# Recurrence, router, experts and a feed-forward layer on one core: the last products of two steps in one run over two column groups

## The chip, the cores and the metric

The kernel runs on one core of a Trainium2 chip. The metric is the device time of one execution in microseconds (us). The core has a matrix engine (TensorE: PE in the rows, and PEld for its weight loads), VectorE (DVE), ScalarE (ACT), GpSimd (POOL) and SyncE (SP), which issues most DMAs. Each engine works through a queue of its own in order; semaphores order the queues against each other.

## The reference, cut to what matters

```python
B, H, S, D = 4, 8, 768, 40
for t in range(S):                     # attention-like recurrence, one 40x40 state per (b, h)
    y[:, :, t] = einsum('bhd,bhde->bhe', r[t], state)
    Sa = einsum('bhde,bhe->bhd', state, a[t])
    state = state * w[t] - outer(Sa, b[t]) + outer(v[t], k[t])
x = y as (3072 tokens, 320)
# mixture of 8 experts: argmax of x @ w_gate picks one; relu(x @ w1[e]) @ w2[e], times the gate
# then a feed-forward layer: h = x @ w_in; maximum(0.01 h, h) @ w_out
```

All of it is in float32 (the weights of the last layer come in float64).

## The kernel before, in words

The program has two parts, one behind the other. The first, `attention`, computes the recurrence in chunks of 32 time steps, and the router's choice for every token. The second, `moe`, computes the experts and the last layer with a written-out order of its own; it is not touched here.

The 768 time steps are cut into 6 blocks (`i`), each of 2 halves (`hf`) of 4 chunks (`g`) of 32. What the code calls a step `s` (0 to 47) is one chunk of one half: `s = 8 i + 2 g + hf`. The two halves are steps of even and odd number; they work on different batches, so that their states don't depend on each other: step `s` needs the state of step `s - 2`. One step treats 16 sequences, as 8 pairs (`p`, with `j` for the member of the pair).

For every chunk `load` brings k, b, a and w, `prep` scales them by running products of w, `gram` makes the 32x32 products within a chunk, `inverse` inverts the triangular matrices of a whole block on VectorE (after a round through DRAM: the copies `mab` are stored in `Md` and loaded as `Mu`), `back` brings the result in as `TB`, and `fix` completes it with many tiny products (lines 488 and 497). `turn` transposes the decays into `Wt` (line 397). A step itself consists of these parts:

- `rv` loads r into a buffer `RE` and v into a buffer `MV`.
- `kbt` transposes k and b (line 524) into `NI` and copies them into the state buffer `Z` as well.
- `chain` is the path from state to state: products at line 554, a copy into X, products at line 565, copies into MV, products at line 581, and the new state into MV of step `s + 2` (line 585).
- `output` transposes MV (line 601) into `Z`, makes r's products with keys (line 614), masks them into `RE` (line 622), and then makes the chunk's rows of y: 16 products, 32 columns wide in weights, 40 wide in the moving operand (line 633, called the py products here). Their results lie in `py`, three PSUM banks; chunk `g` has partitions 32 g to 32 g + 31. Where `g` is 3, the four chunks of a half are complete: VectorE weights them with `Wt` into two of the four buffers `xb` (line 645), and `R.add` routes these 256 tokens: transposes (line 843), logits (854), softmax and places on VectorE, and two scatters on GpSimd (889) that write the tokens into their expert's region `xs`.

The columns of the array that a product uses follow from its output partitions. The 16 py products of a step all use the same group of 32 columns; line 554 puts its products on four such groups in turn, line 581 on the two halves of the partitions in turn.

The order of all this is not the order of the code. Every piece is handed to a planner (`Sched.op`) with a duration, the keys that it reads and writes, and a due time; `Sched.run` places the pieces on the five queues one by one, by its own model of the engines, and `emit` writes them out in that order. Where the planner sees a gap on TensorE, it inserts fillers (line 743: products of constants into an unused corner of `py`), in number a share of the gap. The numbers of buffers (`NRE` for RE, `NZ` for Z, `NWT` for Wt) enter through the keys: a piece that writes a buffer waits for all who read its last content.

Of the kernel before, what the change touches and what calls it, by code (L numbers as in the profile page):

```python
# [239 lines left out]
NMV, NRE, NNI, NZ, NWT = 6, 7, 2, 3, 6  # L240
# [38 lines left out]
def attention(ctx, tc, I, R, eng):  # L279
# [53 lines left out]
    maskZ = cp.tile([TW, XC], F32, name="maskZ")  # L333
# [110 lines left out]
    def inverse(i, parts=(0, 1)):  # L444
# [4 lines left out]
        kM, kT, kt = [[(x, h) for h in parts] for x in ('Mu', 'Tt', 'tmp')]  # L449
# [143 lines left out]
    def output(s):  # L593
# [22 lines left out]
        for j in range(2):  # L616
# [10 lines left out]
            if pm:  # L627
                op('P', .62, lambda E, o=o, j=j: E.tensor_tensor(RE[o:o + 64, j], RE[o:o + 64, j], maskP[o:o + 64].unsqueeze(1).broadcast_to([64, 8, 32]), ALU.mult), ['mask'], [('REs', s % NRE, j, par) for par in range(2)])
        def fy(E):
            for p in range(8):  # L630
                for j in range(2):
                    b, col = place(hf, 2 * p + j)
                    E.matmul(py[32 * g:32 * g + 32, b, col:col + 40], RE[:, j, p, :], Z[:, p, ZC[j]:ZC[j] + 40], start=True, stop=True)  # L633
        op('T', 1.28, fy, zo + [('Zs', s % NZ, j) for j in range(2)] + [('REo', s % NRE, j) for j in range(2)] + [('REs', s % NRE, j, par) for j in range(2) for par in range(2)], [('py', hf, g)], banks=[('py', b) for b in ((0, 1), (1, 2))[hf]], act=2030)
        if g == 3:
            xk = []
            for bb in range(2):
                x = (2 * n + bb) % R.NXB
                xk.append(x)
                u = 8 * bb  # L640
                while u < 8 * bb + 8:
                    b, col = place(hf, u)
                    m = min(8 * bb + 8 - u, 12 - col // 40)
                    op('V', .15 + .0416 * m, lambda E, x=x, u=u, b=b, col=col, m=m, bb=bb:
                       E.tensor_tensor(R.xbs[x][:, 40 * (u - 8 * bb):40 * (u - 8 * bb) + 40 * m], py[:, b, col:col + 40 * m], Wts[n % NWT][:, u:u + m, :].rearrange("p h e -> p (h e)"), ALU.mult),  # L645
                       [('py', hf, k) for k in range(4)] + [('Wt', n % NWT, h, j) for h in range(2) for j in range(2)], [('xb', x, u)], banks=[('py', b)])
                    u += m
            Q.spare = SPF
            R.add(Q, psum, copy, ev, hf, i, xk)
            Q.spare = SPO  # L650
# [50 lines left out]
    for i in range(6):  # L701
# [22 lines left out]
        for c in range(8):  # L724
# [8 lines left out]
            if i == 0 and c < 4:  # L733
                Q.since = ZR0 + ZRS * c
                for e in (2 * c, 2 * c + 1):
                    R.zero_region(Q, e, maskZ, [('X', s % 2)])
# [3 lines left out]
            output(s)  # L740
            Q.spare = 0.
# [27 lines left out]
class Router:  # L769
# [4 lines left out]
    def __init__(self, ctx, tc, I, eng, capacity):  # L774
# [16 lines left out]
        self.tok = cp.tile([128, 1], I32, name="tok")  # L791
# [22 lines left out]
    def setup(self):  # L814
# [4 lines left out]
        P.iota(self.tok, [[0, 1]], base=0, channel_multiplier=1)  # L819
# [10 lines left out]
    def add(self, Q, psum, copy, ev, hf, blk, xk):  # L830
# [55 lines left out]
        for i, x in enumerate(xk):  # L886
            op('P', .18, lambda E, i=i, x=x: E.tensor_scalar(self.xbs[x].bitcast(I32)[:, D:D + 1], self.tok, (2 * hf + i) * 768 + blk * 128, None, ALU.add), ['rconst'], [('xbt', x)])
# [558 lines left out]
```

## Time and profile before

| what | us |
|---|---|
| median of 3 runs (1145.17 to 1154.86) | 1154.43 |
| the profiled execution | 1154.42 |
| its span, first to last instruction | 1152.6 |
| TensorE busy, fillers included | 1037.0 |
| VectorE / ScalarE / GpSimd busy | 729.0 / 553.9 / 303.9 |
| fillers (line 743), 1161 of them | 82.8 |
| first load of scattered tokens issued, the end of the recurrence | 560.28 |

The profile is that of one execution. Busy times are of the whole span; a stretch of it can look quite different. Matrix records come in pairs of a weight load and a product, and a product in float32 has two records of each kind.

### The profile page before, as it was taken

To read this page: it belongs to the slowest core of one execution; us is meant where nothing else is said; L and a number is where in the kernel's file an instruction comes from. 1 tells how busy PE (TensorE), PEld (TensorE's weight loads), DVE (VectorE), ACT (ScalarE), POOL (GpSimd) and SP (SyncE) were. 2 spreads that over 40 slices of the span, in tenths; PEclk is the share of its full clock that TensorE was granted. 3 is DMA by queue.
4 is the path that set the end of the run, shared out by engine and by line. 5 is a ranking of instruction groups with operands and counts; after the bars stand their busy time and mean duration, and the time that the engine had idled before them with its cause. 6 is when DMAs were issued, how large, how long until landed. Compare 5 with 4: busy or idle time off the path is not lost.

```text
span 1152.6 us, 39205 instructions
## 1 busy us (share of the span) xinstructions
PE 1037.0 (90%) x17036; PEld 929.2 (81%) x17036; DVE 729.0 (63%) x1613; ACT 553.9 (48%) x1269; POOL 303.9 (26%) x279
## 2 busy tenths in 40 slices
PE   5786987998978989899589999999999999999997
PEld 4675776887866877778579889889989999999997
DVE  8884684985966955434477787786764545444453
ACT  5133654855836836667344434444533333333343
POOL 6000011002002001010145565673749191010100
PEclk9988897998989979989799999999999999999999
DMA  7757566464554722430466666653311010000000
GB/s 182 200 142 191 144 143 196 135 138 142 130 141 125 184 61 72 96 96 6 142 213 197 190 196 201 203 175 122 92 35 49 21 36 12 12 14 10 24 13 15
DMA packets 146244, 129.59 MB, mean 112 GB/s; under 512 B 102288, under 2 KB 110736, under 8 KB 146064
## 3 DMA queue, kind: packets, MB, share of 16 engines
q1 hardware_dynamic: 143760, 119.11, 37.6%
q0 software_dynamic: 2304, 7.89, 1.9%
q8 instruction: 136, 2.23, 0.8%
q14 instruction: 44, 0.36, 0.1%
HBM read 102.13 MB, written 24.85 MB: 110 GB/s over the span
## 4 chain that ended last, share of the span: by engine, by line
PE 55%; issue 17%; DVE 8%; ACT 8%; DMA 6%; POOL 4%; SPq 2%; DVEq 0%; POOLq 0%; ACTq 0%
PE ph L1000 13%; PE py L633 5%; PE py L743 4%; PE ch L581 3%; PE tr L601 3%; ACT Z L297 3%; PE oy L1207 2%; PE oy L1206 2%; PE oy L1205 2%; PE tr L397 2%; PE tr L415 2%; PE tr L497 2%; DMA wc<-cvm 2%; PE tr L614 2%; ACT NI L297 2%
## 5 line engine op out<-in xcount | busy, mean ns | idle before, releaser
L1000 PE MATMUL ph<-xt,wq 128*128 128x512 f32 (+2 forms) x1408 | 311.8, 365 | 4.9 <-DVE xt L1041 4.9
L1000 PEld LDWEIGHTS ph<-xt,wq 128*128 128x128 f32 x1408 | 248.4, 190 | 35.0 <-DVE xt L1041 6.0
L1185 DVE TENSOR_TENSOR gf<-gf,ph 128x512 f32<-128x512 f32 (+1 forms) x112 | 68.3, 610 | 99.0 <-ACT gf L1184 92.6
L889 POOL DMA_INDIRECT xs<-xb,rii x24 | 28.8, 1199 | 371.6 <-DVE rii L879 260.8
L1189 DVE TENSOR_TENSOR gl<-gf,gh 128x512 fp32r<-128x512 f32 (+1 forms) x112 | 76.7, 685 | 70.0 <-ACT gh L1188 70.0
L1184 ACT ACTIVATE gf<-ph 128x512 f32<-128x512 f32 (+1 forms) x112 | 60.0, 535 | 109.6 <-PE ph L1000 107.0
L1188 ACT CAST gh<-gf 128x512 fp32r<-128x512 f32 (+1 forms) x112 | 62.7, 559 | 96.4 <-DVE gf L1185 95.0
L297 ACT COPY Z<-tr 40x512 f32<-40x512 f32 (+1 forms) x192 | 97.7, 539 | 20.9 <-PE tr L601 19.1
L1051 ACT ACTIVATE gh<-ph 128x448 fp32r<-128x448 f32 x64 | 34.9, 545 | 118.7 <-PE ph L1000 118.7
L1207 PE MATMUL oy<-wo,gl 128*128 128x320 f32 x288 | 89.2, 310 | 0.1
L1206 PE MATMUL oy<-wo,gh 128*128 128x320 f32 x288 | 88.9, 309 | 0.0
L1205 PE MATMUL oy<-wo,gh 128*128 128x320 f32 x288 | 88.8, 308 | 0.0
L743 PE MATMUL py<-one 128*128 128x128 bf16 x1161 | 82.8, 224 | 3.2 <-DVE xb L645 1.6
L1215 POOL DMA_INDIRECT out_dram<-ob,gid x24 | 23.9, 995 | 218.5 <-ACT ob L1214 213.3
L622 DVE TENSOR_TENSOR RE<-tr,maskP 64x128 f32<-64x128 f32 x192 | 55.1, 287 | 35.6 <-PE tr L614 28.0
L585 DVE TENSOR_TENSOR MV<-ch,WC 40x320 f32<-40x320 f32 x92 | 44.9, 488 | 50.3 <-PE ch L581 42.6
L743 PEld LDWEIGHTS <-one 128*128 128x128 bf16 x1161 | 69.9, 100 | 8.0 <-issue 3.6
L1065 PE MATMUL y<-gh,wo 128*128 128x448 f32 x192 | 73.1, 381 | 2.9 <-DVE Y L1072 2.9
L633 PE MATMUL py<-Z,RE 128*32 128x40 f32 x1536 | 69.9, 212 | 2.1 <-issue 2.1
L1068 PE MATMUL y<-gl,wo 128*128 128x448 f32 x192 | 70.6, 368 | 0.0
L633 PEld LDWEIGHTS py<-Z,RE 128*32 128x32 f32 x1536 | 64.3, 120 | 5.9 <-issue 2.7
L430 DVE TENSOR_TENSOR AE<-tr,maskP 32x128 f32<-32x128 f32 x176 | 49.9, 284 | 28.6 <-PE tr L415 17.8
(170 smaller groups left out, 2140.8 us busy)
## 6 DMA issues: line engine op xcount, KB each, us to landing
KB<-in_kbT_dram SPq DMA_DIRECT2D x24, 512.0 KB
RE<-in_rT_dram SPq DMA_DIRECT2D x48, 256.0 KB
AE<-in_aT_dram SPq DMA_DIRECT2D x20, 512.0 KB
raw<-in_wo_dram SPq DMA_DIRECT2D x16, 640.0 KB
raw<-in_wqa_dram SPq DMA_DIRECT2D x16, 512.0 KB
w<-in_wT_dram SPq DMA_DIRECT2D x24, 264.0 KB
xs<-maskZ SPq DMA_DIRECT2D x8, 563.5 KB
win<-xs SPq DMA_DIRECT2D x8, 563.5 KB
```

The lines of the kernel that those rows point to most:

```text
L297: (E.copy if E is A else E.tensor_copy)(o, i)
L633: E.matmul(py[32 * g:32 * g + 32, b, col:col + 40], RE[:, j, p, :], Z[:, p, ZC[j]:ZC[j] + 40], start=True, stop=True)
L743: Q.emit(lambda: T.matmul(py[:, 2, 320:448], R.one, R.one, start=True, stop=True))
L1000: T.matmul(ph, l, r, start=k == 0, stop=k == 7)
L1065: T.matmul(y[c], hi, gh, start=m == 0, stop=False)
L1068: T.matmul(y[c], hi, gl, start=False, stop=m == 7)
L1185: V.tensor_tensor(gf, gf, ph, ALU.max)
L1188: A.copy(gh, gf)
L1189: V.tensor_tensor(gl, gf, gh.bitcast(F32), ALU.subtract)
L1205: T.matmul(o, gh[:, sl], w[:, 0:320], start=m == 0, stop=False)
L1206: T.matmul(o, gh[:, sl], w[:, 320:640], start=False, stop=False)
L1207: T.matmul(o, gl[:, sl], w[:, 0:320], start=False, stop=m == 15)
```

## The change

The py products leave `output` and go into a new function `sums`, which is called behind the `output` of every odd step and treats that step and the one before. It alternates between the two steps, product by product. For the second half (`hf` 1) the chunks' place in `py` is turned by two (chunk `g` has partitions 32 ((g + 2) mod 4) on), so that the two steps use different column groups. The decays (`turn`) are turned in the same way, and so are the token numbers (a second column of `tok`). The weighting and the routing of both halves come behind the last pair of a block. Since RE and Z of the even step now live until the odd step's products, the numbers of buffers change: RE from 7 to 6, Z from 3 to 4, Wt from 6 to 5. Room for the fourth Z is also made by two tiles that no longer exist by themselves: `tmp` lies in `Ta`, and `maskZ`, the rows that initialize the experts' regions, in the fourth `xb`.

```diff
-NMV, NRE, NNI, NZ, NWT = 6, 7, 2, 3, 6
+NMV, NRE, NNI, NZ, NWT = 6, 6, 2, 4, 5
...
-    tmp = cp.tile([128, 112], F32, name="tmp")
     Ta = cp.tile([128, 16, 16], F32, name="Ta")
+    tmp = Ta.rearrange("u a b -> u (a b)")
...
-    maskZ = cp.tile([TW, XC], F32, name="maskZ")
+    maskZ = R.xbs[3][0:TW]
...
-                        o = 32 * ((g + 0) % 4)
+                        o = 32 * ((g + 2 * hf) % 4)
...
+    def sums(s):
+
+        i, g, _, _ = info(s)
         def fy(E):
             for p in range(8):
                 for j in range(2):
-                    b, col = place(hf, 2 * p + j)
-                    E.matmul(py[32 * g:32 * g + 32, b, col:col + 40], RE[:, j, p, :], Z[:, p, ZC[j]:ZC[j] + 40], start=True, stop=True)
-        op('T', 1.28, fy, zo + [('Zs', s % NZ, j) for j in range(2)] + [('REo', s % NRE, j) for j in range(2)] + [('REs', s % NRE, j, par) for j in range(2) for par in range(2)], [('py', hf, g)], banks=[('py', b) for b in ((0, 1), (1, 2))[hf]], act=2030)
+                    for hf in range(2):
+                        b, col = place(hf, 2 * p + j)
+                        q = 32 * ((g + 2 * hf) % 4)
+                        x, z = REs[(s + hf) % NRE], Zs[(s + hf) % NZ]
+                        E.matmul(py[q:q + 32, b, col:col + 40], x[:, j, p, :], z[:, p, ZC[j]:ZC[j] + 40], start=True, stop=True)
+        keys = []
+        for u in (s, s + 1):
+            keys += [('Zo', u % NZ, h, j) for h in range(2) for j in range(2)] + [('Zs', u % NZ, j) for j in range(2)]
+            keys += [('REo', u % NRE, j) for j in range(2)] + [('REs', u % NRE, j, par) for j in range(2) for par in range(2)]
+        op('T', 1.45, fy, keys, [('py', hf, g) for hf in range(2)], banks=[('py', b) for b in range(3)], act=4000)
         if g == 3:
+            for hf in range(2):
+                n = 2 * i + hf
...
             output(s)
+            if s % 2:
+                sums(s - 1)
...
-        self.tok = cp.tile([128, 1], I32, name="tok")
+        self.tok = cp.tile([128, 2], I32, name="tok")
...
+        for o in (0, 64):
+            P.iota(self.tok[o:o + 64, 1:2], [[0, 1]], base=64 - o, channel_multiplier=1)
```

The loops of the weighting (line 645) and the call of `R.add` are the same as before but for the loop over `hf`. The pieces that write the experts' regions take the keys of the fourth `xb` as read.

## Rows read from the trace of the kernel before

**Rows 1.** Part 1 of the page: busy time, share of the span, instructions.
```profile
PE 1037.0 (90%) x17036; PEld 929.2 (81%) x17036; DVE 729.0 (63%) x1613; ACT 553.9 (48%) x1269; POOL 303.9 (26%) x279
```
**Rows 2.** Chain that ended last, by line: 120 to 545 us, then 366 to 393.
```profile
by line: issue 12.1%; PE py L633 11.9%; PE tr L601 6.9%; ACT Z L297 6.8%; PE ch L581 6.7%; PE py L743 5.4%; PE tr L497 4.4%; PE tr L614 4.4%; PE tr L397 4.2%; PE tr L415 4.1%; PE tr L524 4.0%; ACT NI L297 3.6%; PE tr L488 3.5%; PE ch L565 3
...
by line: ACT Z L297 17.3%; PE py L633 14.0%; PE tr L601 10.3%; PE ch L581 8.8%; ACT NI L297 8.5%; DVE AE L430 8.5%; PE py L743 6.6%; PE tr L524 4.6%; PE tr L614 4.6%; ACT MV L297 4.2%; PE ch L554 3.7%; PE ch L565 3.1%; issue 2.8%; PE tr L41
```
**Rows 3.** Windows, quiet (clock behind POOL), their sum; sum of 242:284, 321:366, 401:448.
```profile
284.00:311.00 27.00, 26.14 (x709) 22.86 (x707) 24.12 (x70) 22.60 (x60) 0.00 (x0) 0.98 0.54 128
366.00:393.00 27.00, 26.39 (x746) 22.71 (x748) 24.13 (x66) 23.90 (x63) 0.00 (x0) 1.00 0.62 151
448.00:478.00 30.00, 28.96 (x814) 24.94 (x813) 19.31 (x65) 25.78 (x71) 0.00 (x0) 1.00 0.50 107
511.00:546.00 35.00, 33.98 (x922) 29.03 (x920) 14.96 (x48) 29.49 (x79) 0.00 (x0) 1.00 0.17 51
sum 119.00, PE 115.47 PEld 99.54 DVE 82.52 ACT 101.77 POOL 0.00; mean PE 28.87 PEld 24.88 DVE 20.63 ACT 25.44 POOL 0.00
...
sum 134.00, PE 110.13 PEld 95.22 DVE 80.11 ACT 62.77 POOL 24.03; mean PE 36.71 PEld 31.74 DVE 26.70 ACT 20.92 POOL 8.01
```
**Rows 4.** Windows of line 743 alone: sum of the same four quiet stretches.
```profile
sum 119.00, PE 11.25 PEld 8.96; mean PE 2.81 PEld 2.24
```
**Rows 5.** Waits of PE, 120 to 545 us: total, times, longest.
```profile
PE tr L497 <- issue: 17.9, 15, 4.1
PE tr L488 <- issue: 9.4, 11, 3.1
```
**Rows 6.** Part 3 of the page, PE's instruction queue: packets, MB, share.
```profile
q8 instruction: 136, 2.23, 0.8%
```
**Rows 7.** Timeline of PE, 371 to 393 us: start, length with the last one's end.
```profile
374.35 0.81 PE L581 MATMUL ch<-MV,NI 128*40 128x40 f32 x32
375.09 1.33 PE L633 MATMUL py<-Z,RE 128*32 128x40 f32 x32
...
378.98 0.49 PE L554 MATMUL ch<-MV,AE 128*32 128x40 f32 x32
379.40 0.64 PE L601 MATMUL tr<-ident,MV 128*104 128x128 f32 x4
...
381.33 1.33 PE L633 MATMUL py<-Z,RE 128*32 128x40 f32 x32
382.59 0.66 PE L524 MATMUL tr<-ident,KB 128*128 128x128 f32 x4
```
**Rows 8.** Windows of line 633 alone: sums of the quiet and busy stretches.
```profile
sum 119.00, PE 27.99 PEld 25.48; mean PE 7.00 PEld 6.37
...
sum 134.00, PE 10.84 PEld 10.10; mean PE 3.61 PEld 3.37
```
**Rows 9.** Timeline of DVE behind the last py products.
```profile
546.06 0.49 DVE L645 TENSOR_TENSOR xb<-py,Wt 128x320 f32<-128x320 f32 x1 [0.84 <-PE py L633]
```
**Rows 10.** The chain in order of time, 538 to 568 us.
```profile
542.02 0.66 PE tr L843 x6
...
550.16 2.60 PE py L743 x43
```
**Rows 11.** Timeline of POOL, 540 to 560 us: idle before, in brackets.
```profile
550.27 1.07 POOL L889 DMA_INDIRECT xs<-xb,rii  x1 [44.16 <-DVE rii L879]
...
556.24 2.28 POOL L889 DMA_INDIRECT xs<-xb,rii  x1 [0.30 <-issue]
```
**Rows 12.** Waits of SP's queue, whole span: total, times, longest.
```profile
SPq L349 <- PE py L633: 30.0, 12, 6.1
```
**Rows 13.** Timeline of SP, 366 to 412 us.
```profile
389.39 0.35 SPq L349 DMA_DIRECT2D RE<-in_rT_dram  x1
389.84 6.58 SPq L349 DMA_DIRECT2D Md<-mab  x8
```
**Rows 14.** Part 5 of the page: busy, mean ns, idle before.
```profile
L633 PE MATMUL py<-Z,RE 128*32 128x40 f32 x1536 | 69.9, 212 | 2.1 <-issue 2.1
```

More of the change, by code (lines that the diff above doesn't have):

```diff
@@ L448, in inverse @@
         H, C = slice(o, o + n), range(4 * parts[0], 4 * parts[-1] + 4)
-        kM, kT, kt = [[(x, h) for h in parts] for x in ('Mu', 'Tt', 'tmp')]
+        kM, kT, kt = [[(x, h) for h in parts] for x in ('Mu', 'Tt', 'Ta')]
         U = slice(o // 4, (o + n) // 4)
@@ L631, in fy @@
                 for j in range(2):
-                    b, col = place(hf, 2 * p + j)
-                    E.matmul(py[32 * g:32 * g + 32, b, col:col + 40], RE[:, j, p, :], Z[:, p, ZC[j]:ZC[j] + 40], start=True, stop=True)
-        op('T', 1.28, fy, zo + [('Zs', s % NZ, j) for j in range(2)] + [('REo', s % NRE, j) for j in range(2)] + [('REs', s % NRE, j, par) for j in range(2) for par in range(2)], [('py', hf, g)], banks=[('py', b) for b in ((0, 1), (1, 2))[hf]], act=2030)
-        if g == 3:
[L636 to L650, printed above, removed]
@@ new lines, in sums @@
+        op('T', 1.45, fy, keys, [('py', hf, g) for hf in range(2)], banks=[('py', b) for b in range(3)], act=4000)
+        if g == 3:
+            for hf in range(2):
+                n = 2 * i + hf
+                xk = []
+                for bb in range(2):
+                    x = (2 * n + bb) % R.NXB
+                    xk.append(x)
+                    u = 8 * bb
+                    while u < 8 * bb + 8:
+                        b, col = place(hf, u)
+                        m = min(8 * bb + 8 - u, 12 - col // 40)
+                        op('V', .15 + .0416 * m, lambda E, x=x, u=u, b=b, col=col, m=m, bb=bb, n=n:
+                           E.tensor_tensor(R.xbs[x][:, 40 * (u - 8 * bb):40 * (u - 8 * bb) + 40 * m], py[:, b, col:col + 40 * m], Wts[n % NWT][:, u:u + m, :].rearrange("p h e -> p (h e)"), ALU.mult),
+                           [('py', hf, k) for k in range(4)] + [('Wt', n % NWT, h, j) for h in range(2) for j in range(2)], [('xb', x, u)], banks=[('py', b)])
+                        u += m
+                Q.spare = SPF
+                R.add(Q, psum, copy, ev, hf, i, xk)
+                Q.spare = SPO
@@ L735, in attention @@
                 for e in (2 * c, 2 * c + 1):
-                    R.zero_region(Q, e, maskZ, [('X', s % 2)])
+                    R.zero_region(Q, e, maskZ, [('X', s % 2), ('xbt', 3), ('xbg', 3)] + [('xb', 3, u) for u in range(16)])
                 Q.since = 0.
@@ L818, in setup @@
         P.memset(self.acc, 0.0)
-        P.iota(self.tok, [[0, 1]], base=0, channel_multiplier=1)
+        P.iota(self.tok[:, 0:1], [[0, 1]], base=0, channel_multiplier=1)
+        for o in (0, 64):
+            P.iota(self.tok[o:o + 64, 1:2], [[0, 1]], base=64 - o, channel_multiplier=1)
         for e in range(NE):
@@ L886, in add @@
         for i, x in enumerate(xk):
-            op('P', .18, lambda E, i=i, x=x: E.tensor_scalar(self.xbs[x].bitcast(I32)[:, D:D + 1], self.tok, (2 * hf + i) * 768 + blk * 128, None, ALU.add), ['rconst'], [('xbt', x)])
+            op('P', .18, lambda E, i=i, x=x: E.tensor_scalar(self.xbs[x].bitcast(I32)[:, D:D + 1], self.tok[:, hf:hf + 1], (2 * hf + i) * 768 + blk * 128, None, ALU.add), ['rconst'], [('xbt', x)])
             def fs(E, i=i, x=x):
```

## The prediction

> **What bounds the kernel now.** I read the page's first part, then the chain that ended last by line and by stretch, then windows of engine times, then the matrix engine's timeline. TensorE is busy for most of the span [rows 1]. The change lies in the recurrence (until about 546 us; behind it comes the expert part, which is not edited). There the chain shows the py products (line 633) as its costliest line of work, 11.9% of 425 us, beside 12.1% "issue" [rows 2]. The recurrence has stretches of two kinds, and both kinds must be priced.
>
> In the quiet stretches (the later steps of a block) TensorE is busy for 115.47 of 119 us, at full clock (2.4 GHz) in three of the four [rows 3]. 11.25 us of that are fillers (line 743), which compute nothing that is used [rows 4], so needed work is 104.2 us. The other engines are as full: adding for each stretch the fuller of VectorE and ScalarE gives 24.12 + 24.13 + 25.78 + 29.49 = 103.5 us [rows 3]. Three engines are level here; the chain passes through ScalarE and VectorE copies for nearly two fifths (17.3 + 8.5 + 8.5 + 4.2%) [rows 2].
>
> In the busy stretches (the inverse is put together, two chunks are turned, Gram products run) TensorE is busy for 110.13 of 134 us [rows 3], and what ends its idle time in the recurrence is mostly "issue": 17.9 us ahead of line 497, 9.4 us ahead of line 488 [rows 5]. TensorE's 34,072 products and weight loads [rows 1] came with 136 packets of its instruction queue [rows 6], one per 250 instructions. The gaps stand where lines of many tiny products run. I read them as TensorE waiting for its own instructions. The change keeps their number.
>
> **The change part by part.** (1) The py products. A step's run is 16 products (32 records, two passes each), all on one group of 32 columns. Start to start it takes 382.59 - 381.33 = 1.26 us [rows 7], so two steps cost 2.52 us. The new run has 32 products that alternate between two groups. Nothing in the trace does just that; two neighbours bound it. Line 554 has the same shape on four groups in turn: 379.40 - 378.98 = 0.42 us for 16, so 0.84 us for 32. Line 581 has 16 products of 40 moving columns on two halves in turn, 375.09 - 374.35 = 0.74 us, so 1.48 us for 32 [rows 7]. The other end is no overlap, 2.52 us. I take 1.48 us, since line 581 is nearest (two groups): 1.04 us less for a pair, 0.52 us for a step, 25 us for 24 pairs at full clock; the bounds are 40 us and nothing. The Trainium skill ("TensorE: Matmul & The Clock Gate", Packing small matmuls) says that tiles in different column groups run concurrently, some 4 ns apart; worked out from that as an estimate, a pair would cost little more than one run, about 1.3 us, and 24 pairs would free some 30 us in place of 25. Line 581 agrees that two groups overlap, but not that fully.
>
> How much of it arrives? Quiet: 27.99 us of py products are 21 steps [rows 8]; 21 x 0.52 = 10.9 us go. Of four runs between 366 and 393 us (4 x 1.26 = 5.04 us) the chain holds 14.0% of 27 us = 3.8 us [rows 2], three quarters, so 8.2 us could arrive. But then ScalarE or VectorE would have to be 103.5 / 110.8 = 93% busy where it is 87% now, and what they wait for next is each other; besides, fillers are put where the order leaves gaps, and will take part of the room. I take two fifths, 3.3 us, 0.16 us a step (ends: nothing and 8.2 us). Busy: six steps cost 10.84 us [rows 8], 1.8 us each and so dearer than the 1.26 us above; 1.04 / 2.52 of it, 4.5 us, go. Where the next stop is a wait for instructions, TensorE only waits longer for them, because a pair asks for the same instructions in less time. I take a third, 1.5 us, 0.25 us a step (ends: nothing and 4.5 us). The other 21 steps are of both kinds: 0.2 us each, 4.2 us. Together 9.0 us.
>
> (2) The end of the recurrence. Before, the router's work for the first half starts right behind its own last products, a step ahead of the second half. Now both begin after the last pair. Taken away: the single run of 1.26 us ahead of the last one. Added behind it: the first half's weighting on VectorE (two pieces like the one of 0.49 us [rows 9], 1.0 us), its transposes (0.66 us [rows 10]) and logits on TensorE, and four scatters on GpSimd in one row, where two and two stand apart now. At 1.07 us each and 0.30 us between them [rows 11] four take 5.2 us; from near 550 us, where the first starts now, they would end near 555.5 us, while the last now starts at 556.24 us and takes 2.28 [rows 11]. Besides, 2.60 us of fillers stand in this tail and may shrink [rows 10]. So the ends are -3 and +4 us (the added pieces in full, with a second such row of copies and logits, and nothing given back). I take +1.5 us, the weighting and the transposes less a little. What follows the last scatter stays.
>
> (3) Buffers. State buffers (Z) go from three to four: an even step's copy into Z still waits for the products of the step three before, as now, and an odd step's for earlier ones; nothing. Six of r (RE) in place of seven: the load for an even step waits for the products of the step five before in place of seven, for an odd one six. Quiet steps are 119 / 21 = 5.7 us apart [rows 3, 8], so over 25 us stay for a load that is needed a moment ahead of its step's products; no cost, unless the queue blocks (last rival). Five Wt in place of six: the second of a block's turned decays waits for the first half's weighting of the block before, some step later than it could now; it is needed eight steps on. The rotation by two groups, the second column of token numbers and the sharing of tmp and maskZ with other tiles change places, not work: nothing.
>
> Sum: 9.0 less 1.5 is 7.5 us. The profiled execution took 1154.42 us (span 1152.6 and 1.8 around it), the same as the median of the runs, 1154.43: **1147 us**, own range 1141 to 1153.
>
> **The rivals.** *All of it arrives.* For: the products are on the chain nearly everywhere, and quiet TensorE idles for only 3.5 us. Against: the level engines and the waits for instructions. 25 us less the tail: 1154.4 - 25 + 1.5 = 1131 us. The Trainium skill ("Runtime: NRT & Kernel Launch", Instruction fetch mechanics) says that the fetching of instructions is hidden behind their issue; by that, the busy stretches would pay in full too. The waits by "issue" [rows 5] speak against it. Chance 0.15.
>
> *None of it arrives.* Fillers go into the gaps, ScalarE and VectorE set the quiet steps, instructions the busy ones; only the tail is left: 1156 us. Chance 0.22.
>
> *Slower, through the DMA queue.* SyncE issues in order and already waits 30.0 us, 12 times, for py products [rows 12]; behind a load of r stand stores of the Gram blocks (Md at 389.84 us, right behind RE at 389.39) [rows 13]. They feed the load of Mu, and so the inverse and all of the busy stretch. If a load of r stands ahead of Md and its pair ends a step later than the single run did, Md is up to 5.7 us late; in half of the five blocks that is 14 us, with the tail 1170 us. It decides from the point at which the load's buffer is released after the Gram blocks are copied out. Chance 0.18. Against it: the order of the queue is made with that wait known.
>
> **How the numbers follow.** Forecast 0.45. Below 1142.9 us (faster by over 1%, about what a measurement of this kernel tells from no change) lie the first rival and a quarter of the forecast's weight: 0.15 + 0.12 = 0.27. Above 1166 us lies most of the last: 0.16. The rest, 0.57, is within 1%. The range runs from the first rival's 1131 us to 1167 us, which leaves out the far half of the last one and the bound of 40 us.
>
> **What would show it.** A pair of 64 records in about 1.48 us start to start, its two tiles alternating; line 633's busy time down from 69.9 us [rows 14] to some 40 us; quiet stretches shorter by about 3%, with ScalarE or VectorE above 90% and the chain's share through them up; "issue" as large as before or larger in the busy stretches; fillers in the quiet stretches no fewer than now [rows 4]; four scatters in one run at the end. The prediction fails if the pair costs over 2 us, if the stretches shrink by all that is removed, if SyncE's waits for line 633 grow well beyond 30 us with the Gram stores behind them, or if the new order of the queues moves something that I don't name.

## The result, and the profile after

The changed kernel takes 1166.53 us (median of 4 runs, 1164.97 to 1168.55), the kernel before beside it 1150.78 us: a ratio of 1.0132 with a 95% interval of 1.0098 to 1.0166. The forecast was 1147 us, faster. The change makes the kernel about 15 us slower, where the forecast had it 7 us faster. In microseconds 1166.53 lies at the upper edge of the wide range (1131 to 1167) and outside the narrow one (1141 to 1153); but the range was worked out from 1154.4 us, 12.6 us below its upper end, and the measured step is 15.8 us. The profiled execution of the changed kernel took 1168.55 us, its span is 1166.8 us.

The expert part did not change: from the first load of scattered tokens to the end of the span it is 1152.6 - 560.3 = 592.3 us before and 1166.8 - 574.2 = 592.6 us after. The 14 us lie in the recurrence: its last py products end at 557.5 us instead of 546.0 (+11.5), and the tail from there to the first load grew from 14.3 to 16.7 us (+2.4).

The page's first part, its instruction queue, and the groups of the py products (now line 640) and of the fillers (now line 758), which answer to [rows 1, 6, 14]:

```profile
PE 1029.6 (88%) x17257; PEld 921.8 (79%) x17257; DVE 726.4 (62%) x1601; ACT 560.6 (48%) x1282; POOL 299.9 (26%) x282
...
q8 instruction: 138, 2.26, 0.8%
...
L758 PE MATMUL py<-one 128*128 128x128 bf16 x1382 | 97.3, 226 | 2.6 <-DVE xb L658 1.4 <-POOL one L802 1.2
...
L640 PE MATMUL py<-Z,RE 128*32 128x40 f32 x1536 | 35.9, 210 | 9.7 <-issue 9.7
```

The pairs do what they should: the same 1536 records keep TensorE busy for 35.9 us instead of 69.9 [rows 14]. But TensorE's sum falls by 7.4 us only, since 221 more fillers take 14.5 us and other groups 12.1 us more. In the timeline a pair stands on TensorE as one row of 64 records (start, length, line, idle before in brackets):

```profile
527.77 1.34 PE L640 MATMUL py<-Z,RE 128*32 128x40 f32 x64
529.04 0.66 PE L524 MATMUL tr<-ident,KB 128*128 128x128 f32 x4
...
537.06 0.81 PE L581 MATMUL ch<-MV,NI 128*40 128x40 f32 x30 [0.21 <-ACT MV L297]
539.30 0.27 PE L581 MATMUL ch<-MV,NI 128*40 128x40 f32 x2 [1.44 <-issue]
539.50 1.34 PE L640 MATMUL py<-Z,RE 128*32 128x40 f32 x64
540.77 0.66 PE L524 MATMUL tr<-ident,KB 128*128 128x128 f32 x4
```

Start to start a pair takes 529.04 - 527.77 = 1.27 us, as long as one of the runs that it replaces (1.26 us, [rows 7]).

The windows of the quiet stretches, between the same steps as in [rows 3] (the first four rows and their sum; then the sums of line 640 and of line 758 alone), and the sums of the busy ones (all, and line 640):

```profile
291.80:318.40 26.60, 23.87 (x717) 20.18 (x717) 23.43 (x71) 23.91 (x64) 0.00 (x0) 1.00 0.50 118
376.50:403.50 27.00, 26.25 (x780) 22.49 (x782) 23.79 (x70) 22.01 (x59) 0.00 (x0) 0.97 0.50 119
457.20:482.90 25.70, 23.33 (x664) 19.28 (x663) 17.24 (x60) 22.64 (x60) 0.00 (x0) 0.94 0.38 84
516.00:557.50 41.50, 36.49 (x1132) 31.22 (x1131) 15.69 (x49) 32.35 (x88) 3.00 (x6) 1.00 0.25 66
sum 120.80, PE 109.94 PEld 93.17 DVE 80.15 ACT 100.91 POOL 3.00; mean PE 27.49 PEld 23.29 DVE 20.04 ACT 25.23 POOL 0.75
...
sum 120.80, PE 13.46 PEld 12.25; mean PE 3.37 PEld 3.06
...
sum 120.80, PE 16.53 PEld 14.17; mean PE 4.13 PEld 3.54
...
sum 132.50, PE 105.12 PEld 91.91 DVE 70.66 ACT 62.52 POOL 23.23; mean PE 35.04 PEld 30.64 DVE 23.55 ACT 20.84 POOL 7.74
...
sum 132.50, PE 6.80 PEld 6.23; mean PE 2.27 PEld 2.08
```

This is the reading that the forecast lacked. In the quiet stretches the py products fall from 27.99 to 13.46 us [rows 8], and the stretches get 1.8 us longer (119.0 to 120.8). TensorE's idle time, the stretch less its busy time, rises from 3.5 to 10.9 us, the fillers from 11.25 [rows 4] to 16.53, and the other products by 3.7 us. So what the pairs free turns into waiting and fillers, and into other products that take longer. (The records, 640 after and 672 before, show that one run of the 21 lies outside these stretches now; that is 1.3 us of the 14.5.) The busy stretches get 1.5 us shorter (134.0 to 132.5) for 4.0 us of py products less. The other 11 us lie outside both kinds: 4.8 us ahead of the first busy stretch, which begins at 246.8 us instead of 242, and 5.9 us in the one step behind the second quiet stretch (403.5 to 417.4 us, before 393 to 401).

The chain that ended last, 120 to 556 us by line, three of TensorE's waits and SyncE's wait for the py products answer to [rows 2, 5, 12]:

```profile
by line: issue 15.8%; ACT Z L297 9.7%; PE tr L601 5.9%; PE py L758 5.4%; PE ch L581 5.2%; ACT NI L297 4.6%; PE py L640 4.4%; PE tr L524 4.1%; PE tr L497 4.1%; ACT MV L297 4.1%; PE tr L614 4.0%; PE tr L397 3.9%; PE tr L415 3.5%; PE tr L488 3
...
PE py L640 <- issue: 9.7, 4, 4.1
PE tr L488 <- issue: 8.8, 6, 2.9
PE tr L497 <- issue: 8.0, 6, 2.3
...
SPq L349 <- PE py L640: 16.7, 7, 5.6
```

The py products' share of the chain falls from 11.9% to 4.4%; "issue" (12.1 to 15.8%) and the copies into Z (6.8 to 9.7%) take its place. GpSimd's four scatters at the end do stand in one row, as in the forecast's tail [rows 11]:

```profile
566.47 1.07 POOL L906 DMA_INDIRECT xs<-xb,rii  x1 [45.74 <-DVE xb L902]
...
570.39 2.03 POOL L906 DMA_INDIRECT xs<-xb,rii  x1 [0.31 <-issue]
```

### The profile page after: what moved, and what is told of

Its sections match the earlier page's. It is cut to its first block, busy times and chain, and to the rows that moved or that the text cites. A ratio compares the mean times of both kernels' runs of the same rounds, so it can differ in the third digit from the quotient of the medians.

```text
span 1166.8 us, 39681 instructions
## 1 busy us (share of the span) xinstructions
PE 1029.6 (88%) x17257; PEld 921.8 (79%) x17257; DVE 726.4 (62%) x1601; ACT 560.6 (48%) x1282; POOL 299.9 (26%) x282
## 4 chain that ended last, share of the span: by engine, by line
PE 55%; issue 14%; ACT 10%; DVE 10%; DMA 6%; POOL 5%; SPq 1%; POOLq 0%; DVEq 0%; ACTq 0%
PE ph L1017 14%; PE py L758 5%; ACT Z L297 4%; PE oy L1224 3%; PE oy L1223 3%; PE oy L1222 3%; PE tr L601 2%; PE tr L397 2%; PE ch L581 2%; ACT NI L297 2%; PE tr L415 2%; PE py L640 2%; PE tr L497 2%; DMA wc<-cvm 2%; PE tr L524 2%
## 5 line engine op out<-in xcount | busy, mean ns | idle before, releaser
L297 ACT COPY Z<-tr 40x512 f32<-40x512 f32 x192 | 98.0, 540 | 30.6 <-PE tr L601 29.0
L758 PE MATMUL py<-one 128*128 128x128 bf16 x1382 | 97.3, 226 | 2.6 <-DVE xb L658 1.4
L758 PEld LDWEIGHTS <-one 128*128 128x128 bf16 x1382 | 83.7, 101 | 7.9 <-issue 3.1
L1232 POOL DMA_INDIRECT out_dram<-ob,gid x24 | 23.9, 995 | 218.5 <-ACT ob L1231 213.3
L622 DVE TENSOR_TENSOR RE<-tr,maskP 64x128 f32<-64x128 f32 x192 | 55.1, 287 | 30.7 <-PE tr L614 27.4
L601 PE MATMUL tr<-ident,MV 128*104 128x128 f32 x384 | 63.9, 307 | 5.0 <-issue 3.5
L430 DVE TENSOR_TENSOR AE<-tr,maskP 32x128 f32<-32x128 f32 x176 | 49.9, 284 | 26.8 <-PE tr L415 13.5
L297 ACT COPY NI<-tr 64x160 f32<-64x160 f32 x192 | 55.1, 287 | 22.6 <-PE tr L524 19.2
```

The source lines that it names most:

```text
L297: (E.copy if E is A else E.tensor_copy)(o, i)
L601: E.transpose(c['t'][0:104, q, :], MV[:, 4 * h + q], ident)
L758: Q.emit(lambda: T.matmul(py[:, 2, 320:448], R.one, R.one, start=True, stop=True))
```

## The experiments

Every ratio is to the kernel before on the same chip, with its 95% interval; 0.01 is 11.5 us. The first theory was that the pairs cost by their instructions: 128 of them, the weight loads and products of two runs, in half the time, so that TensorE waits for its next ones behind them. The runs did not bear it out, and the later ones weigh others; each expectation says which.

**The parts of the change by themselves.** The changed kernel without the pairing alone: every step has its own run again, on the rotated groups, with the new buffers and with both halves routed at the block's end.

```diff
-            if s % 2:
-                sums(s - 1)
+            sums(s - s % 2, s % 2)
...
+        def single(s, hf):
+            def fy(E):
+                for p in range(8):
+                    for j in range(2):
+                        b, col = place(hf, 2 * p + j)
+                        q = 32 * ((g + 2 * hf) % 4)
+                        E.matmul(py[q:q + 32, b, col:col + 40], REs[s % NRE][:, j, p, :], Zs[s % NZ][:, p, ZC[j]:ZC[j] + 40], start=True, stop=True)
...
+            op('T', 1.28, fy, keys, [('py', hf, g)], banks=[('py', b) for b in ((0, 1), (1, 2))[hf]], act=2030)
+        single(s + part, part)
```

> The changed kernel without the pairing alone: the py products stay a run of their own for each step, behind its output, planned at 1.28 us; the chunks turned by two, the buffers and the routing of both halves behind the block's last products are the change's. Theory: what costs is the pairing, so this lies near the kernel with the buffers alone, 1146 to 1156 us (the routing of both halves at the end may add 2 us). Rival F (the routing at the end, or the turned chunks, cost): 1160 us or more.

Measured: 1144.18 us, 0.9967 [0.9934, 1.0000]. Rotation, buffers and late routing together cost nothing that shows; the pairing costs 1.0132 - 0.9967, about 19 us. The kernel before with the new buffer numbers and shared tiles alone agrees.

```diff
-NMV, NRE, NNI, NZ, NWT = 6, 7, 2, 3, 6
+NMV, NRE, NNI, NZ, NWT = 6, 6, 2, 4, 5
```

> The kernel before with the change's buffer numbers alone (RE 6, Z 4, Wt 5, tmp in Ta, maskZ in the fourth xb); products, pairs and routing as before. Theory A: buffers cost nothing, 1147 to 1156 us. Rival C (the buffers are what costs: loads of r wait longer on SyncE): 1160 us or more.

Measured: 1148.82 us, 0.9944 [0.9911, 0.9976]: a small gain.

Since any edit gives the planner another order, one weight of it was changed for both kernels, to see what an order is worth.

```diff
-    SLACK, PATIENCE, ALPHA = 0.075, 61.165, 0.105
+    SLACK, PATIENCE, ALPHA = 0.075, 50.0, 0.105
```

> The changed kernel with one weight of the planner, PATIENCE, at 50 instead of 61.165: the same operations with the same dependencies, in another order from the fifth block on. The output is the reference's. Theory A (the pair itself costs, by its instructions or as a lump): another order costs about as much as this one, 1160 to 1175 us, ratio to the kernel before 1.008 to 1.02. Theory O (the order that the planner happened to find for the paired kernel is a bad one, and the pair itself is worth the 9 us that were forecast): another order lands anywhere between 1140 and 1170 us, and one under 1150 us would speak for it.

> The unpaired kernel with the planner's weight PATIENCE at 50 instead of 61.165: the same operations in another order. The output is the reference's. The paired kernel in another order took 1.0150 of the kernel before, the unpaired one in its first order 0.9967. Theory P (the pairing costs, whatever the order): 1143 to 1156 us, ratio 0.99 to 1.005, 10 us or more below the paired kernel in another order. Theory O (the orders differ by luck, and the pairing by itself costs nothing): anywhere between 1145 and 1175 us, and 1165 us or more would speak for it.

Measured: paired 1171.86 us, 1.0150 [1.0091, 1.0208]; unpaired 1143.88 us, 0.9971 [0.9945, 0.9997]. The pairing costs 19 to 21 us in either order. By the expectation these orders differ from the fifth block on only; a further kernel below, whose pairs are planned longer, is in another order from early on and comes to 1.0141. An unlucky order is thus not the likely cause.

**The overlap by itself.** The pair with its two halves one behind the other, so that they don't overlap; order and waits are those of the changed kernel.

```diff
-            for p in range(8):
-                for j in range(2):
-                    for hf in range(2):
+            for hf in range(2):
+                for p in range(8):
+                    for j in range(2):
```

> The changed kernel with the order of all queues kept, but inside each pair the first step's 16 products come first and then the second's, so that two products in a row share a column group again. Theory A (what the overlap frees is lost to waits for TensorE's instructions): a pair takes about 2.5 us in place of 1.28, line 640 costs some 30 us more, and nearly all of that comes out of the waits that end 1.2 to 1.5 us after an instruction packet (67 us in the changed kernel, below 50 here); the time stays within 1160 to 1173 us. Rival B (TensorE's time counts, and the new order of the queues is what costs): 24 pairs x 1.25 us = 30 us more, 1190 to 1197 us.

Measured: 1176.98 us, 1.0195 [1.0154, 1.0236], between the two ranges. Its py products take 63.0 us:

```profile
L640 PE MATMUL py<-Z,RE 128*32 128x40 f32 x1536 | 63.0, 212 | 5.2 <-issue 5.2
```

So the overlap frees 63.0 - 35.9 = 27.1 us, and about 0.63% or 7 us of it arrives (the intervals just overlap, so the 7 is rough). Gathering two steps' products behind the second, with no overlap at all, costs 1.0195 - 0.9967, some 26 us over the unpaired kernel. The loss is in the gathering, not in the overlap. To let the planner reckon with the longer duration, the changed kernel was ordered as if a pair took 2.56 us:

```diff
-        op('T', 1.45, fy, keys, [('py', hf, g) for hf in range(2)], banks=[('py', b) for b in range(3)], act=4000)
+        op('T', 2.56, fy, keys, [('py', hf, g) for hf in range(2)], banks=[('py', b) for b in range(3)], act=4000)
```

> The changed kernel with a single number changed: the planner is told that a pair takes 2.56 us in place of 1.45, so that it makes another order with more room behind each pair, while the pair itself runs as fast as in the changed kernel. Theory E (the order that the planner makes around a pair sets the time, not TensorE's time): the time moves by 10 us or more against the changed kernel, most likely up to 1175 to 1190 us, though TensorE's work is the same. Theory A (waits for instructions and fillers): room behind each pair lets the instructions catch up, the waits behind packets fall below 55 us and the time stays within 1160 to 1170 us.

Measured: 1164.19 us, 1.0141 [1.0076, 1.0207]. The longer duration in the plan makes no difference that shows.

**Fillers.** A sixth as many, each a float32 product of 192 columns, in the changed kernel and in the one before; then none in either.

```diff
-            for _ in range(self.fill.get(i, 0)):
+            for _ in range((self.fill.get(i, 0) + 3) // 6):
```

> The changed kernel, the order of all else kept, with fillers of another kind: in float32 over 192 columns, a sixth as many, so that a filler's time needs about a third of the instructions (1382 x 2 = 2764 records before, some 900 after). Theory A: about 1850 instructions fewer are 7 packets; at 3.3 us a packet up to 24 us, of which I expect 10 to 20: 1147 to 1157 us, waits behind packets below 55 us. Rival B (the order of the queues): no change, 1163 to 1170 us.

> The kernel before with the same lighter fillers. Theory A: some 1550 instructions fewer, 6 packets, 20 us at most; 1137 to 1147 us, waits behind packets well below the 45 us of the kernel before. Rival B: no change, 1147 to 1155 us.

> The changed kernel, order kept, with no fillers at all. Theory A (fillers took the room that the pairs freed: 61.5 us of TensorE's time in the recurrence against 49.2 before): 5 to 15 us faster than the changed kernel, 1152 to 1162 us, if the lower clock costs less than the fillers do. Rival D (fillers stand in gaps that are there anyway, and keep the clock up): slower than the changed kernel, 1170 to 1190 us, with more of the recurrence at the lower clock than 118 us.

> The kernel before with no fillers, for comparison with the changed one without them. Theory A: no better than the kernel before by more than 5 us, 1148 to 1160 us, so that the difference between the two kernels shrinks without fillers. Rival D: slower, 1160 to 1180 us, and the difference of 13 us between the two stays.

Measured: light fillers after 1167.83 us, 1.0151 [1.0096, 1.0205], and before 1149.90 us, 0.9978 [0.9957, 0.9999]; none after 1162.42 us, 1.0125 [1.0049, 1.0200], and none before 1133.84 us, 0.9848 [0.9759, 0.9936]. The kernel before without fillers is faster than both of its theories had it. Taking the fillers out does not give back the loss of the changed kernel, and against the unpaired kernel without them (0.9939, below) the pairing still costs 1.9%, some 21 us. So neither the fillers' instructions nor their time are what the pairs lose.

**Instructions in a short time.** Behind each unpaired run 32 tiny products (64 instructions), and as a control one long product with four.

```diff
+                for _ in range(32):
+                    E.matmul(py[0:32, 2, 320:321], R.one[0:32, 0:32], R.one[0:32, 0:1], start=True, stop=True)
```

```diff
+                E.matmul(py[:, 2, 320:512], ident, ident[:, 0:96].unsqueeze(1).broadcast_to([128, 2, 96]), start=True, stop=True)
```

> The unpaired kernel (1144.2 us) with 32 products of 32 by 32 by 1 behind each of its 48 runs of py products: 64 instructions more per run, 3072 in all, and little TensorE work. The output is the reference's. Theory A (a run of py products puts so many instructions into so short a time that TensorE then has to wait for its next ones): the instructions lie as close together as in a pair, so the waits after the runs come back. 48 waits of 0.3 to 0.6 us and the 48 times 0.3 us of the products themselves: 1160 to 1185 us, ratio to the kernel before 1.01 to 1.03, and the gaps of TensorE that end about 1.3 us after a 16 KB instruction packet sum to 50 to 65 us where the unpaired kernel has 37. Theory B (the number of instructions in a short time doesn't matter; the pair costs because it is one piece of work that must stand whole in TensorE's order): 1144 to 1155 us, like its control with one long product, and the gaps stay at 35 to 42 us.

> The control of the run with tiny products: the unpaired kernel with one float32 product of 192 columns (2 products and 2 weight loads as the profile counts them, about 0.3 us) behind each run of py products: about the same TensorE time added, and hardly any instructions. The output is the reference's. Both theories: 48 times 0.3 us is 14 us of TensorE work, of which some two fifths arrives in the end time: 1144 to 1152 us, ratio 0.995 to 1.002. Theory A expects it 10 to 30 us below the run with tiny products, theory B within 5 us of it.

Measured: tiny 1194.04 us, 1.0369 [1.0306, 1.0432]; long 1167.04 us, 1.0105 [1.0050, 1.0161]. Both lie above their expected ranges; both expectations had the size of the added work wrong. In the timelines (first the kernel with tiny products, then the one with the long product) start to start it is not 0.3 us:

```profile
507.26 0.95 PE L641 MATMUL py<-one 32*32 32x1 bf16 x32
508.14 0.50 PE L614 MATMUL tr<-RE,Z 128*64 128x64 f32 x9
```

```profile
484.29 0.59 PE L640 MATMUL py<-ident 128*128 128x192 f32 x2
484.81 0.81 PE L581 MATMUL ch<-MV,NI 128*40 128x40 f32 x32
```

The tiny ones take 0.88 us a run, 42 us in 48 runs, and the time rises by 1.0369 - 0.9967, 46 us, 1.1 for each us added. The long ones take 0.52 us, 25 us in all, and 16 us arrive, 0.64 for each. By the intervals the tiny ones cost 38 to 54 us, the long ones 8 to 23, so that the tiny ones cost about their whole time, and that they cost more than it is not shown. These runs also differ in two things at once, work and instructions, and so don't tell whether pairs suffer by it. The same long product behind each pair does:

> The changed kernel with one float32 product of 192 columns behind each of the 24 pairs: two passes, 0.52 us together behind the unpaired runs, 12.5 us in all, and four instructions. The output is the reference's. Theory S (behind each pair TensorE waits for its next instructions, so work without instructions fits into that wait): 0 to 4 us more than the changed kernel: 1166 to 1171 us, ratio 1.012 to 1.017. Theory D (TensorE's time costs as elsewhere; behind the unpaired runs 25 us of the same product brought 16 us): 8 us more, 1172 to 1180 us, ratio 1.018 to 1.026.

```profile
536.39 0.59 PE L641 MATMUL py<-ident 128*128 128x192 f32 x2
536.82 0.60 PE L524 MATMUL tr<-ident,KB 128*128 128x128 f32 x4
```

Measured: 1168.21 us, 1.0201 [1.0157, 1.0245]. If TensorE waited for instructions behind each pair, the 24 products (0.43 us in this row, 0.52 in the one above, so 10 to 12.5 us) would have fitted into that wait. About 0.69% or 8 us arrive, by the ratio as theory D had it and as large a part as behind unpaired runs (the intervals leave room for 1 to 14 us). The supply of instructions is not shown to be the loss of the pairs.

**Late, or together.** First the unpaired kernel in which the even step's run also waits for Z and RE of the odd step. Both runs are pieces of their own.

```diff
-            sums(s - s % 2, s % 2)
+            if s % 2:
+                sums(s - 1, 0)
+                sums(s - 1, 1)
...
+            if not hf:
+                u = s + 1
+                keys += [('Zo', u % NZ, h, j) for h in range(2) for j in range(2)] + [('Zs', u % NZ, j) for j in range(2)]
+                keys += [('REo', u % NRE, j) for j in range(2)] + [('REs', u % NRE, j, par) for j in range(2) for par in range(2)]
```

> The unpaired kernel, in which the first step's run of 32 py products has to wait, as in the pair, for the Z and RE of the second step too; both runs stay apart, each its own operation, so that other work may stand between them. The output is the reference's. Theory D (the cost of the pair is that the first step's products come a step later, as work that could have filled a gap of TensorE and then stands in front of other products): most of the cost of the pair run one half after the other (1.0195) comes back: 1162 to 1178 us, ratio 1.010 to 1.022. Theory L (the cost is the length of one uninterrupted run of 64 products, 128 instructions): 1144 to 1153 us, ratio 0.995 to 1.002, as unpaired.

Measured: 1173.26 us, 1.0209 [1.0150, 1.0268]. One added wait on half of the runs, with no pair and no overlap, brings the whole loss of the gathered kernel (1.0195). The two runs come free at the same moment, and the planner puts them into one place: in the timeline they stand as one row of 64 records, as 22 of the 24 pairs of runs do:

```profile
532.08 2.37 PE L639 MATMUL py<-Z,RE 128*32 128x40 f32 x64
534.37 0.66 PE L524 MATMUL tr<-ident,KB 128*128 128x128 f32 x4
...
543.42 0.39 PE L581 MATMUL ch<-MV,NI 128*40 128x40 f32 x10 [0.85 <-issue]
543.73 2.37 PE L639 MATMUL py<-Z,RE 128*32 128x40 f32 x64
```

Where the time goes can be counted step by step. A step begins with its products at line 554. The windows below are sums over blocks 1 to 5, of the 20 intervals from an even step's beginning to the odd one's, and of the 15 from an odd step's to the next even one's within a block; of all work, and of the py products alone. First the unpaired kernel, even intervals, then odd ones:

```profile
sum 181.10, PE 165.97 PEld 142.76 DVE 124.95 ACT 132.58 POOL 23.38; mean PE 8.30 PEld 7.14 DVE 6.25 ACT 6.63 POOL 1.17
sum 181.10, PE 21.69 PEld 19.61; mean PE 1.08 PEld 0.98
...
sum 151.20, PE 132.61 PEld 116.19 DVE 93.58 ACT 81.99 POOL 9.89; mean PE 8.84 PEld 7.75 DVE 6.24 ACT 5.47 POOL 0.66
sum 151.20, PE 28.76 PEld 26.39; mean PE 1.92 PEld 1.76
```

The same with the even step's run made late:

```profile
sum 216.90, PE 193.97 PEld 170.50 DVE 145.98 ACT 141.37 POOL 22.22; mean PE 9.70 PEld 8.53 DVE 7.30 ACT 7.07 POOL 1.11
sum 216.90, PE 38.23 PEld 36.10; mean PE 1.91 PEld 1.81
...
sum 159.10, PE 120.46 PEld 104.29 DVE 84.79 ACT 77.42 POOL 10.69; mean PE 8.03 PEld 6.95 DVE 5.65 ACT 5.16 POOL 0.71
sum 159.10, PE 11.22 PEld 10.73; mean PE 0.75 PEld 0.72
```

And the changed kernel:

```profile
sum 200.90, PE 172.93 PEld 147.88 DVE 135.43 ACT 134.04 POOL 9.00; mean PE 8.65 PEld 7.39 DVE 6.77 ACT 6.70 POOL 0.45
sum 200.90, PE 20.45 PEld 18.53; mean PE 1.02 PEld 0.93
...
sum 164.70, PE 125.54 PEld 107.74 DVE 85.65 ACT 86.14 POOL 26.78; mean PE 8.37 PEld 7.18 DVE 5.71 ACT 5.74 POOL 1.79
sum 164.70, PE 8.36 PEld 7.55; mean PE 0.56 PEld 0.50
```

The odd intervals lose 28.76 - 11.22 = 17.5 us of py products when the even step's run is late, and get no shorter (151.2 to 159.1): TensorE's idle time in them goes from 18.6 to 38.6 us. The even intervals gain 16.5 us of py products and grow by 35.8. In the changed kernel the odd intervals lose 20.4 us of py products and grow by 13.5 (idle 39.2 us); the even ones have about the same py products as unpaired (20.45) and grow by 19.8, 12.8 of it idle time. The unpaired kernel's profiled execution is 8 us below its median, so each of these differences is some us too large; in the other order (1141.35 us for its profiled execution, 2.5 below its median) the unpaired intervals sum to 182.9 and 154.4 us, and the picture is the same.

Next, all 48 runs one step late, each alone again.

```diff
-            sums(s - s % 2, s % 2)
+            for v in ([s - 1] if s else []) + ([s] if s == 47 else []):
+                sums(v - v % 2, v % 2)
...
+            if s < 47:
+                u = s + 1
```

(The keys of u are added as above.)

> The unpaired kernel, in which each of the 48 runs of py products waits, besides its own step's Z and RE, for those of the step behind it, so that all are a step late but still one run per step. The output is the reference's. With the first step's run alone made late (two runs in every second step, none in the other) it was 1.0209 of the kernel before. Theory D1 (the cost is that both runs come into the same one of two steps, which grows longer while the other, whose gaps they had filled, does not grow shorter): 1144 to 1156 us at a kernel before of 1148, ratio 0.995 to 1.007. Theory D2 (the cost is lateness itself: products that wait longer for their inputs have less freedom to fill gaps, and hold Z and RE longer): at least as slow as with every second run late, ratio 1.015 to 1.035.

Measured: 1151.88 us, 1.0037 [1.0002, 1.0071], in the range of D1. In blocks 0 to 3 the first half's weighting here reads the decays of a later block (the number of Wt buffers was not raised with the delay), so the expectation's second sentence does not hold. Number and size of the operations are the same, but what a kernel with one Wt buffer more would take was not measured. Its timeline has single runs, with other work between them (in one place three runs stand together):

```profile
513.13 1.31 PE L639 MATMUL py<-Z,RE 128*32 128x40 f32 x32
516.58 1.33 PE L639 MATMUL py<-Z,RE 128*32 128x40 f32 x32
```

The lateness by itself, and the longer time for which Z and RE are held, thus cost 1.0037 - 0.9967, 8 us, of the 28 us; the other 20 (12 to 28 by the intervals) come only where both runs come free at the same moment. But D1 named a wrong reason: of the intervals' py products 37.28 us stand in the even ones here too, which grow as before (214.5 us), and yet the odd ones get shorter (135.2 us):

```profile
sum 214.50, PE 37.28 PEld 33.55; mean PE 1.86 PEld 1.68
...
sum 135.20, PE 118.02 PEld 102.02 DVE 82.11 ACT 88.20 POOL 24.20; mean PE 7.87 PEld 6.80 DVE 5.47 ACT 5.88 POOL 1.61
```

What costs is therefore rather the two runs in one place than their standing in every second interval. The last test cuts the changed kernel's pair into two pieces of 32 records, both still overlapped:

```diff
-            for p in range(8):
+            for p in range(4 * half, 4 * half + 4):
...
-        op('T', 1.45, fy, keys, [('py', hf, g) for hf in range(2)], banks=[('py', b) for b in range(3)], act=4000)
+        for half in range(2):
+            op('T', .73, lambda E, half=half: fy(E, half), keys, [('py', hf, g) for hf in range(2)], banks=[('py', b) for b in range(3)], act=2000)
```

> The changed kernel with each pair cut into two operations of 32 products, both half over one another as before (about 0.65 us and 64 instructions each), so that other work may stand between them. The output is the reference's. Theory L or S (the cost is the length of one uninterrupted run, by what stands behind it or by the supply of its 128 instructions): 1145 to 1158 us, ratio 0.995 to 1.005, 8 us or more below the changed kernel. Theory D (the cost is that the first step's products come late): as the changed kernel, 1162 to 1172 us, ratio 1.010 to 1.018.

Measured: 1156.54 us, 1.0081 [1.0045, 1.0118], between the two theories: 0.5% or 6 us of the loss come back (the intervals overlap, so the 6 is rough). In 20 of the 24 pairs the halves do stand apart in the trace.

**The fastest version.** The unpaired kernel, and the kernel before with the buffers of the change, each without fillers.

> The unpaired kernel with no filler products in the work before the experts. The output is the reference's. Theory A (fillers are instructions that TensorE has to be supplied with, and with short runs the supply sets the time): the kernel before gained about 15 us when its fillers went (1149 to 1134), and so does this: 1125 to 1135 us, ratio 0.978 to 0.988. Theory B (without fillers the lower clock stretches the products, and the unpaired kernel has less idle time to hide it in): 1138 to 1150 us, ratio 0.99 to 1.0.

> The kernel before with the buffer numbers alone of the change (0.9944) and without its filler products (which alone took the kernel before to 0.9848): the candidate for the fastest. The output is the reference's. If the two gains add up: ratio 0.976 to 0.984. If the buffers gain only by another order of the same instructions, whose idle time the missing fillers change anyway: 0.983 to 0.995.

Measured: 1148.07 us, 0.9939 [0.9905, 0.9974], and 1136.83 us, 0.9916 [0.9883, 0.9949]. The gains don't add up. The lowest ratio is that of the kernel before without fillers (0.9848); its interval, 0.9759 to 0.9936, holds the second of these too, so which is fastest is not settled.

## Why the prediction was wrong

**The step that failed** is the lower end of what arrives: "ends: nothing and 8.2 us" in the quiet stretches, "nothing and 4.5 us" in the busy ones. It took the pairs as runs that got shorter in their old places. But the even step's run leaves its place, and it is queued behind the odd step's Z and RE, where it stands together with the odd step's run. I priced that wait at its buffers and at the tail, and put its cost in the steps at nothing without a reason. It is worth 26 to 28 us (1.0195 and 1.0209 against 0.9967), about as much as the overlap frees (27.1 us), of which only some 7 arrive. 8 us of it are the lateness (1.0037), the other 20 come with both runs in one place. The profile of before had a warning: a run of 1.26 us stood in each step among products that wait for copies by ScalarE and VectorE, and TensorE idled for only 3.5 of 119 us [rows 3, 7]. That such runs kept the idle time so low is my reading of these rows.

**The pair's price** was mis-sized in the good direction: 1.27 us instead of 1.48. Line 581 was the worse neighbour, and line 633's busy time fell by 34.0 us, not 25. The Trainium skill ("TensorE: Matmul & The Clock Gate", Packing small matmuls) says that tiles in different column groups run concurrently; the estimate of 1.3 us that was worked out from it agrees with the trace's 1.27.

**What arrives of it**: I took 9.0 of 25 us. Against the gathered kernel without overlap 7 of 27 us arrive, 0.27 where I took 0.36 (the intervals leave 1 to 13 us); that is the smaller error. The gathering had no term. So the sum is 7 us gained and some 26 lost, 19 us slower than unpaired. The rotation, the buffers and the late routing together come to 0.9967, with an interval that reaches 1.0000, where the forecast had +1.5 us for the tail and nothing for the buffers; in the traces the tail did grow, by 2.4 us.

**The rivals.** "None of it arrives" (1156 us) named the right mechanism for part of it: fillers took 5.3 us of the quiet stretches' 14.5, idle time 7.3. The one on the slower side was the wrong one: SyncE's waits for py products fell from 30.0 us, 12 times [rows 12], to 16.7 us, 7 times. Other waits of SyncE did grow (for the transposes of line 601 from 53.3 to 73.8 us), but little of them is on the chain: from 120 to 556 us it passes through 4.0 us of DMA work, nearly all of it one load of v,

```profile
395.77 3.95 DMA MV<-in_vt_dram
```

and in the gathered kernel without overlap, which is slower, through none. So the order of that queue is at most a small part of the loss.

**What would show it.** "Issue" did grow in the chain of the whole recurrence, and TensorE's idle time in the busy stretches from 23.9 to 27.4 us; the copies' share went up, the fillers became more, and the scatters stand in one row, as I wrote. The quiet stretches did not shrink by 3%, and neither VectorE nor ScalarE is above 90% busy (80.15 and 100.91 of 120.8 us), though the py products are half of what they were. That level engines set the quiet steps is therefore not the whole story: they wait longer.

**What stays open**: why two runs in one place cost about 20 us more than runs that stand apart. A pair holds TensorE no longer than a single run does (1.27 against 1.26 us), and cutting it in halves gives back only some 6 us, so the length of one uninterrupted run is a part of it at most. The longer idle time and the larger share of time at the lower clock go with it (mean granted clock of the profiled executions 0.936 after and 0.935 with the even step's run late, 0.948 unpaired and with all runs a step late), but no run sets the clock apart from the idle time. That the rows' "issue" waits hang on the supply of instructions was not shown for the pairs, and not refuted for the tiny products. These waits do not follow the time: "issue" is 10.4% of the chain in the unpaired kernel (120 to 525 us), 15.8% in the changed one, but 13.6% in the slower one without overlap (120 to 570 us) and 14.1% with all runs a step late (120 to 544 us), which is hardly slower than before.

## What to carry to other kernels

Before two pieces of work are joined for a better rate, price the places that they stand in. As I read these runs, a short independent run between dependent products fills a wait; when it has to come free together with a second one, it leaves that wait empty and lengthens another. What is shown is the price: 8 us for coming late, and 20 more for coming together. Test the joining and the overlap apart, by running the joined piece without overlap; here that one run showed that the overlap was worth 7 us and the joining cost 26. And neither a freed us nor an added one counts in full: about 0.27 of the pairs' saving arrived, and about 0.64 of the long products' time (the intervals are too wide to tell these two apart).

## What the runs showed of the hardware

Two runs of 32 records on column groups two apart take 1.27 us, as long as one (1.26 us), so the second costs TensorE next to nothing when products alternate. Where the two follow each other on the same two groups, they take 2.29 us (534.37 - 532.08, above). 32 products of 32 by 32 by 1 with their weight loads take 0.88 us, 27 ns for each, where a record of the py products, with 40 columns, takes 39 ns (1.26 us for 32); in time they cost 46 us for 42 us added, where two passes of 192 columns cost 16 for 25. In the kernel before, fillers cost more than they bring: without them it goes to 0.9848 [0.9759, 0.9936]. In three other kernels their removal makes no difference that shows (1.0125 against 1.0132 in the changed one, 0.9939 against 0.9967 unpaired, 0.9916 against 0.9944 with the new buffers), though a larger part of the recurrence then runs at the lower clock (in the changed kernel the mean granted clock falls from 0.936 to 0.900).
